# A gate behind the last value load, and mode 63 taken through the channel matrix by itself, in four column groups and two PSUM halves, with tables for units 0 to 3

## The chip, the cores and the metric

The kernel runs on one core of one Trainium2 chip. The metric is device time in microseconds (us) for one launch, from a call to its end. A profile is one execution recorded by the hardware; its span goes from the first to the last instruction of the program. In all texts PE is the matrix engine (PEld its weight loads), DVE the vector engine, ACT the scalar engine, POOL the GpSimd engine and SP the sync engine, which here only issues DMAs.

## The reference

Two layers stand one behind the other. The first is attention with a window of 128 and an ALiBi slope for each head; the second mixes the tokens in the frequency domain and applies a channel matrix.

```python
# q, k, v: (8 batches, 8 heads, 576 tokens, 64), fp32; w_r, w_i: (64, 512, 512); w_ch: (512, 512)
scores = where((rel >= 0) & (rel < 128), q @ k.T / 8 - slope * abs(rel), -1e9)
x = softmax(scores) @ v                       # laid out as (8, 576, 512)
X = rfft(x, axis=1)                           # over the tokens
Yr = einsum('bmd,mde->bme', Xr, w_r) - einsum('bmd,mde->bme', Xi, w_i)   # the first 64 modes
Yi = einsum('bmd,mde->bme', Xr, w_i) + einsum('bmd,mde->bme', Xi, w_r)
u = x + irfft(Yr + 1j * Yi, n=576)
out = u + maximum(u @ w_ch, 0)                # (8, 576, 512), fp32
```

The two mode weights are 64 x 2 matrices of 512 x 512 in fp32, 134 MB in all, and are read once. The output is 9.44 MB.

## The kernel before

**Attention** runs over 16 work units, a batch and a half of the heads each. `STAGE` is a list, written by hand, of steps with a lag; the loop over `stage` goes through it and so fixes the order of instructions on every engine. `cast("v", u)` turns the raw values into bf16 and then issues the load of unit u + 2 on SP's queue (`load`, lines 211 and 215). Behind each stage, POOL issues loads of mode weights: `AHEAD` says how many go into the `early` tiles in stages 1 to 13, `LATER` how many go into `spare` tiles, which are the raw buffers of q, k and v, in stages 12 to 15. Before the load of `AHEAD`, POOL copies one element of `x` that the stage before has just written, into `gate` (line 556). The copy has no other use than that POOL's queue waits there. The weights are cast from fp32 to bf16 on their way, which is why they are issued from POOL.

**The mode weights** are streamed next. The 64 modes go in 16 quads of four (`g`, with `LAST` = 15), and each quad has eight spots (`i`, with `k = 8 * g + i`). A spot of a quad multiplies weight tiles with the spectra in `XC` into the quad's accumulator `acc`, 32 columns of the matrix engine for each mode (line 861). `quad_end` scales and transposes a full accumulator into `YT`. Between the spots the kernel works on what is already there: `stream_spectra` takes finished spectra to rows `Z` and, through the channel matrix `wch`, to rows `ZW`; `project` and `augment` take all tokens through `wch` and add the first 32 modes (`XW`, and `x` in place). `warm` issues three matmuls that nobody reads. The last quad is split. Modes 60 to 62 are summed in `part_acc`, mode 63 in `acc`; `late_end` scales the first 96 rows into `yq`, sends them to rows of `Z` by small DMAs on POOL's queue (`patch`, line 639), and transposes them.

**The end** follows the last weight tile. Its mode's rows are scaled into `yq` by ACT, transposed and copied to `yT` (lines 935 to 940), taken through `wch` together with the other 96 rows (`late_channels`, line 592) into `yw`, and sent by `patch` to rows of `Z` and `ZW`. Then 18 output units follow, a pair of batches and 128 tokens each (two of them hold the last 64 tokens of four batches). For each unit PE fills an accumulator `mm` in `begin` (from `XW`) and `channels` (from `ZW`, with the inverse table `FT`) and an accumulator `yy` in `add_tokens` (from `x`) and `finish_tokens` (from `Z`). ACT writes `r = relu(mm)` in `activate`, DVE writes `o = yy + r` in `finish` (line 817), and SP sends `o` to the output (line 819). Units 0 and 1 (`FIRST`) do not wait for all of the small DMAs: `last_rows` multiplies the rows of `yq` or `yw` directly with a table `FM`, which holds the right rows of `FT` and zeros elsewhere. `FM` is filled with one memset and two DMAs on POOL's queue when the second set of weight buffers is opened. There are two slots of `mm` and `yy` from unit 1 on, and five buffers of `o`.

Of the kernel before, what the change touches and what calls it, by code (L numbers as in the profile page):

```python
# [402 lines left out]
def kernel(  # L403
# [87 lines left out]
    with ExitStack() as actx:  # L491
# [52 lines left out]
        for stage in range(min(lags), n + max(lags)):  # L544
# [8 lines left out]
            if stage in AHEAD:  # L553
                if stage:
                    b, g = at.units[stage - 1]
                    nc.gpsimd.tensor_copy(gate[:1, :1], x[:1, b, 0, 256 * g : 256 * g + 1])  # L556
                load_w(AHEAD[stage], early)
            if stage in LATER:
                load_w(LATER[stage], None)

    with ExitStack() as mctx:
# [8 lines left out]
        lctx, pctx = ExitStack(), ExitStack()  # L570
# [4 lines left out]
        def late_end(acc):  # L575
# [4 lines left out]
            patch([(nc.gpsimd, b) for b in range(2, B)], yq, lambda b: Z[:, b // 2, 1], 0, 6)  # L580
# [8 lines left out]

        def late_channels(zw, yT, yw, c):  # L590
            for et in range(4):
                nc.tensor.matmul(zw[:, c], lhsT=yT[:, et], rhs=wch[:, et, c],  # L592
                                 start=(et == 0), stop=(et == 3))
            nc.scalar.copy(yw[:, c], zw[:, c])
# [40 lines left out]
        def patch(todo, rows, dst, lo=0, hi=8):  # L635

            for queue, b in todo:
                r = 64 * (b % 2) + 8 * (LAST % 8)
                queue.dma_start(out=dst(b)[r + lo : r + hi],
# [6 lines left out]
        def spread(dst, half, b, hf, st, tok, rows=None):  # L646

            row = ROWS[(b % 2) ^ (1 - hf)]
            rows = ZW if rows is None else rows
# [77 lines left out]
        HALVES, FIRST = (0, 1, 2, len(units) - 1), (0, 1)  # L727
# [30 lines left out]
        def late_modes(dst, j, rows):  # L758

            b, st = units[j]  # L760
            for n in range(2):
# [4 lines left out]
                for row in range(2):  # L766
                    spread(dst[:, n], row, b + n, 1, st, row, rows)

        def channels(j):

            late_modes(mms[j][0], j, ZW)

        def last_rows(ps, j, rows):

            st = units[j][1]
            for n in range(2):
                nc.tensor.matmul(ps[:, n], lhsT=FM[:, n, st * P : (st + 1) * P], rhs=rows,  # L777
                                 start=False, stop=True, skip_group_check=True)
# [4 lines left out]
        def activate(j):  # L783

            if j in FIRST:
                last_rows(mms[j][0], j, heads["yw"])
# [13 lines left out]
        def finish_tokens(j):  # L800

            late_modes(yys[j][0], j, Z)

        def finish(j):

            b, st = units[j]
            if j == 0:
                last_rows(yys[0][0], 0, heads["yq"])
            else:
                if j not in yys:  # L810
                    take(j)
                add_tokens(j)
                finish_tokens(j)
            (yy, slot), r = yys.pop(j), rs.pop(j)
            o = heads["out"].tile([P, 2, DM], FP32, tag="o", bufs=5, name="o")
            for c in parts(j):
                nc.vector.tensor_tensor(out=o[:, c], in0=yy[:, c], in1=r[:, c], op=ALU.add)  # L817
# [12 lines left out]
            free.append(slot)  # L830

        quads, side, recycle = [], [], list(again)
        ZW = Z = XW = FM = FC = pairs = wch = w2 = None
        K1 = spot[again[-1]]
        for g in range(NM // 4):
# [5 lines left out]
            for i in range(8):  # L841
                k = 8 * g + i
                if i == 6 and g == LAST:
# [3 lines left out]
                    heads.update(mm=[head], yy=[head])  # L847
                    idle.append(0)
                    free.append(0)
                    begin(0)  # L850
                    channels(0)
                    take(0)
                    add_tokens(0)
                    finish_tokens(0)
                now = turns.pop(0) if turns and spot[turns[0][0]] == k else []
                for a in range(4):
                    for t in now:
                        m, ri = t // 2, t % 2
                        c0 = (a // 2 * 2 * NC + 16 * (1 - ri) + a % 2 * 8) * NM + m
                        into = part_acc if g == LAST and m < NM - 1 else acc  # L860
                        nc.tensor.matmul(  # L861
                            into[32 * (m % 4) : 32 * (m % 4) + 32],
                            lhsT=XC[:, c0 : c0 + 31 * NM + 1 : NM], rhs=wq[t][a],
                            start=(ri == 0 and a == 0), stop=(ri == (m > 0) and a == 3),
                            tile_position=(0, 32 * (m % 4)),
                        )
# [7 lines left out]
                if k == K1:  # L874
# [13 lines left out]
                    FM = right.tile([P, 2, 2 * P], BF16, name="FM")  # L888
                    nc.gpsimd.memset(FM, 0.0)
                    for b in range(2):  # L890
                        nc.gpsimd.dma_start(
                            out=FM.rearrange("(k v) b s -> k v b s", v=16)[:, b, b],
                            in_=FT[64 * b + 56 : 64 * b + 64, b, : 2 * P],
                        )
# [12 lines left out]
                elif g > LAST - 2 and k < 2 * NM - 1 or g == LAST - 2 and not side:  # L907
# [7 lines left out]
            if g == 7:  # L915
# [3 lines left out]
                side.append(partial(augment, len(units) - 1))  # L919
            elif g == LAST - 1:  # L920
# [3 lines left out]
        heads["out"] = mctx.enter_context(tc.tile_pool(name="res", bufs=6, reuse_waits="tile"))  # L924

        yq, yT = heads[LAST]
        zctx = ExitStack()
        zps = zctx.enter_context(tc.tile_pool(name="zps", bufs=1, space=PSUM))
        zl = zps.tile([P, DM], FP32, tag="z0", name="zl")
        nc.tensor.matmul(zl, lhsT=ident, rhs=wch[:, 0], start=True, stop=True)  # L930
        sides = (slice(0, DM // 2), slice(DM // 2, DM))
        trs = (lps.tile([P, 4, P], BF16, tag="tr", name="tr"),
               zps.tile([P, 4, P], BF16, tag="z1", name="tr1"))
        for i, c in enumerate(sides):
            nc.scalar.mul(yq[96:, c], acc[96:, c], 2.0 / S)
# [66 lines left out]
```

## Time and profile before

| | before |
|---|---|
| median of 3 runs | 444.19 us (438.96, 445.89, 444.19) |
| profiled execution | 441.24 us, span 439.4 us |
| mean granted PE clock | 0.847 |
| PE busy | 320.6 us (73%), 3509 matmuls |
| DVE, ACT, POOL busy | 183.7, 162.1, 87.0 us |
| DMA moved | 105.54 MB, 240 GB/s in the mean; POOL's queue 67.22 MB, SP's queue 37.79 MB |
| DMA share, 0 to 135, 141 to 401, 401 to 411, 411 to 437.9 us | 1.05, 1.06, 0.23, 0.97 |
| start of the last weight matmul; first output issue; last two output issues from | 405.27; 410.24; 432.65 us |

The page gives the busy time of each engine, the span in 40 slices, the DMA queues, the chain of work that ended last and the costliest groups of instructions. The DMA share is the busy part of the core's 16 transfer engines, and may come out a little over 1. Bytes are counted as written, so that a weight, read in fp32 and written in bf16, counts half. In a line of the timeline stand the start in us, the duration in us, engine, line of the kernel, operation, and output<-input with its shape; in brackets the idle time before it and what ended it.

### The profile page before, as it was taken

The numbers are of one execution on the slowest core, as the hardware profiler recorded it, in microseconds if no ns is written. First come the engines' busy times: TensorE is split into PE (matmuls) and PEld (weight loads), VectorE is DVE, ScalarE is ACT, GpSimd is POOL, SyncE is SP. The second block draws the span as 40 slices with busy tenths as digits, with TensorE's granted clock in tenths as the row PEclk, the third lists the DMA queues.
The fourth block names the chain that finished last, engine by engine and source line by source line (L and its number), as shares of the span: only waits on it lengthen the run. The fifth ranks groups of instructions, "written<-read, shape, count | busy, mean of one in ns | idle before, by whom it ended". The sixth has DMA issues, their size and how long they took to land. (4 is left out here: it accounts for less than half of the span.)

```text
span 439.4 us, 8314 instructions
## 1 busy us (share of the span) xinstructions
PE 320.6 (73%) x3509; PEld 177.6 (40%) x3509; DVE 183.7 (42%) x332; ACT 162.1 (37%) x211; POOL 87.0 (20%) x162
## 2 busy tenths in 40 slices
PE   4679899969796724553443387999889999698982
PEld 3357577647665411111111133444444444233430
DVE  7689699788783301010000022332222232122684
ACT  6769799987781000000000012323232323101780
POOL 8611011100323101322113111111111110012500
PEclk8679899999999965555555569999999999989997
DMA  8999999999999999999999999999999999997598
GB/s 280 306 329 301 300 292 312 266 302 283 266 224 213 216 214 213 214 213 214 214 213 215 214 214 214 214 215 215 214 214 215 216 213 214 214 215 135 199 368 306
DMA packets 52489, 105.54 MB, mean 240 GB/s; under 512 B 4052, under 2 KB 23396, under 8 KB 52452
## 3 DMA queue, kind: packets, MB, share of 16 engines
q0 software_dynamic: 18992, 67.22, 76.5%
q1 hardware_dynamic: 33460, 37.79, 26.3%
q8 instruction: 27, 0.44, 0.4%
q14 instruction: 10, 0.08, 0.0%
HBM read 162.53 MB, written 9.44 MB: 391 GB/s over the span
## 5 line engine op out<-in xcount | busy, mean ns | idle before, releaser
L861 PE MATMUL acc<-w,XC 128*32 128x512 bf16 x456 | 80.8, 485 | 68.8 <-DMA w<-in_moe_w_i_dram 35.4
L861 PEld LDWEIGHTS <-XC 128*32 128x32 bf16 x508 | 38.7, 148 | 110.1 <-issue 85.0
L297 ACT ACTIVATE att<-sc 128x1024 bf16<-128x1024 f32 x64 | 64.0, 1031 | 10.0 <-PE sc L287 10.0
L627 ACT CAST ZW<-zw 128x512 bf16<-128x512 f32 x8 | 4.7, 586 | 144.7 <-PE zw L625 144.7
L334 PE MATMUL av<-vb,att 128*128 128x132 bf16 (+1 forms) x576 | 38.4, 217 | 11.6 <-DVE x L350 8.8
L599 DVE TENSOR_SCALAR yq<-acc 128x512 bf16<-128x512 f32 x14 | 9.6, 687 | 82.2 <-PE acc L861 82.2
L334 PEld LDWEIGHTS <-att 128*128 128x128 bf16 x704 | 36.6, 98 | 17.2 <-DVE x L350 13.0
L693 PE MATMUL my<-wch,xT 128*64 128x512 bf16 x288 | 34.5, 381 | 5.8 <-ACT x L724 4.3
L702 ACT CAST XW<-my 128x512 bf16<-128x512 f32 x36 | 19.3, 589 | 50.5 <-PE my L650 50.5
L674 DVE COPY xT<-tr 128x1024 bf16<-128x1024 bf16 x18 | 12.5, 692 | 55.0 <-PE tr L672 55.0
L259 ACT COPY qkT<-tp 128x1152 bf16<-128x1152 bf16 x30 | 33.5, 1115 | 5.3 <-PE tp L253 4.5
L481 POOL DMA_DIRECT2D w<-in_moe_w_i_dram x23 | 16.3, 710 | 66.9 <-PE acc L861 44.2
L481 POOL DMA_DIRECT2D w<-in_moe_w_r_dram x22 | 15.6, 709 | 68.5 <-PE acc L861 48.1
L287 PE MATMUL sc<-qkT 64*64 64x256 bf16 (+2 forms) x640 | 25.7, 269 | 2.5 <-ACT qkT L259 1.6
L350 DVE TENSOR_TENSOR x<-av,rec 128x640 bf16<-128x640 f32 x32 | 26.4, 825 | 1.1
L693 PEld LDWEIGHTS <-xT 128*64 128x64 bf16 x288 | 17.1, 109 | 21.6 <-issue 9.2
L817 DVE TENSOR_TENSOR o<-yy,r 128x1024 f32<-128x1024 f32 (+1 forms) x22 | 21.5, 1025 | 4.8 <-DMA Z<-yq 2.6
L236 DVE CAST vb<-vr 64x1024 bf16<-64x1024 f32 x32 | 22.7, 708 | 0.4 <-DMA vr<-in_v_dram 0.2
L287 PEld LDWEIGHTS <-qkT 64*64 64x64 bf16 x640 | 14.8, 110 | 19.8 <-issue 16.5
L556 POOL COPY gate<-x 1x1 bf16<-1x1 bf16 x13 | 5.5, 423 | 86.2 <-DVE x L350 86.2
L724 ACT CAST x<-my 128x512 bf16<-128x512 f32 x18 | 10.6, 586 | 31.0 <-PE my L650 31.0
L274 PE MATMUL sc<-bias,ident 128*128 128x512 bf16 x64 | 20.7, 408 | 1.1 <-ACT att L297 1.1
(134 smaller groups left out, 431.0 us busy)
## 6 DMA issues: line engine op xcount, KB each, us to landing
w<-in_moe_w_i_dram POOLq DMA_DIRECT2D x23, 1024.0 KB, 35.8
w<-in_moe_w_r_dram POOLq DMA_DIRECT2D x22, 1024.0 KB, 35.7
qr<-in_q_dram SPq DMA_DIRECT2D x16, 576.0 KB, 9.2
kr<-in_k_dram SPq DMA_DIRECT2D x16, 576.0 KB, 8.2
vr<-in_v_dram SPq DMA_DIRECT2D x64, 128.0 KB, 7.6
w<-in_moe_w_r_dram POOLq DMA_DIRECT2D x16, 512.0 KB, 14.3
w<-in_moe_w_i_dram POOLq DMA_DIRECT2D x13, 512.0 KB, 24.0
out_dram<-o SPq DMA_DIRECT2D x13, 512.0 KB, 4.6
```

The source lines that it names most:

```text
L236: nc.vector.tensor_copy(self.vb[u % 2][row, :, :, :, W * half : W * half + D], src[row, :2])
L259: (self.nc.vector.tensor_copy if u < 2 and w == "q" else self.nc.scalar.copy)(dst.rearrange("q h (p j) -> q h p j", j=TPP), tp.rearrange(" ...
L274: nc.tensor.matmul(sc[:, e], lhsT=self.ident, rhs=self.bias[:, hv].rearrange("p j n -> p (j n)"), start=True, stop=False, skip_group_check ...
L287: nc.tensor.matmul(sc[64 * half : 64 * half + 64, e, j * 256 + c0 : j * 256 + c0 + n], lhsT=qkT[row, 1, h, k0 + j : k0 + P : 2], rhs=qkT[r ...
L297: self.nc.scalar.activation(self.att[u % 2][:, kt * 8 * P : (kt + 1) * 8 * P], sc.rearrange("p e n -> p (e n)"), AF.Exp, scale=1.0 / math. ...
L334: nc.tensor.matmul(bank[:, qt * W : qt * W + rhs[j].shape[1]], lhsT=att[:, o : o + P], rhs=rhs[j], start=(n == 0 and j == 0), stop=(n == l ...
L350: nc.vector.tensor_tensor(out=self.x[:, b, :, cs].rearrange("p t (h d) -> p h t d", h=2), in0=tiles[:, :, :, :D], in1=rec.unsqueeze(-1).br ...
L481: nc.gpsimd.dma_start(out=t.rearrange("p s a e -> p s (a e)"), in_=w[kinds.pop()][m : m + 2].rearrange("m (p a) e -> p m (a e)", a=4))
L693: nc.tensor.matmul(mm[ROWS[half]], lhsT=lhsT, rhs=wch[:, dt], start=(dt == 0), stop=False, skip_group_check=True,)
L702: nc.scalar.copy(XW[:, j, n], mms[n])
L817: nc.vector.tensor_tensor(out=o[:, c], in0=yy[:, c], in1=r[:, c], op=ALU.add)
L861: nc.tensor.matmul(into[32 * (m % 4) : 32 * (m % 4) + 32], lhsT=XC[:, c0 : c0 + 31 * NM + 1 : NM], rhs=wq[t][a], start=(ri == 0 and a == 0 ...
```

## The change

- In stage 13 POOL copies four elements of the last value unit's raw tile into `gate`, and issues the loads of `LATER[13]` behind it.
- `FM` and a second table `FM3` lie in the part of `YT` that is no longer used. `last_tables` fills them behind quad 11: a memset and four small copies on POOL, ten small DMAs on SP. `fold` is a matrix that adds up four groups of 32 rows.
- `late_end` gets a third part: the 96 rows of modes 60 to 62 go through `wch` ahead of the last weight tile, into `yw`, and their rows of `ZW` for batches 0 and 1 go by SP's queue. The three warming matmuls of spot 125 fall away.
- Mode 63 is summed in two halves of 256 columns in two PSUM tiles (`ends`); ACT scales one half and DVE the other. Then only its 32 rows go through `wch`: each of four column groups takes one quarter of the channels, and the four partial sums in `ywp` are added up by `FM3` for units 0 to 3, and by `fold` for everything else.
- Unit 0 adds `yq` and `yw` by tables; ACT copies its `yy` to `r`, and DVE takes the relu of `mm` in its sum. Units 1 to 3 (`FIRST`) take the rows of modes 60 to 62 from `ZW` (62 of 64 rows) and mode 63 from `FM3`.
- The order of the small DMAs changes; `o` has 7 buffers instead of 5, `r` has 4 instead of 6. Unit 2's `finish` comes before unit 3's `activate`.

```diff
+            if stage == n - 3:
+                nc.gpsimd.tensor_copy(gate[:1, :4], raw["v"][:1, (n - 1) % 2, 1, :, 0])
             if stage in LATER:
                 load_w(LATER[stage], None)
...
             heads[LAST] = yq, yT
-
-        def late_channels(zw, yT, yw, c):
+            yield
+            zl = heads["z"].tile([P, DM], FP32, tag="z0", name="zl")
             for et in range(4):
-                nc.tensor.matmul(zw[:, c], lhsT=yT[:, et], rhs=wch[:, et, c],
+                nc.tensor.matmul(zl[rows], lhsT=yT[:, et, rows], rhs=wch[:, et],
                                  start=(et == 0), stop=(et == 3))
-            nc.scalar.copy(yw[:, c], zw[:, c])
+            nc.scalar.copy(yw[rows], zl[rows])
+            patch(nc.sync, (0, 1), yw, ZW, 0, 6)
...
-        HALVES, FIRST = (0, 1, 2, len(units) - 1), (0, 1)
+        HALVES, FIRST = (0, 1, 2, len(units) - 1), (1, 2, 3)
...
             if j in FIRST:
-                last_rows(mms[j][0], j, heads["yw"])
+                if j not in mms:
+                    begin(j)
+                channels(j, 62)
+                last_rows(mms[j][0], j, ywp, FM3)
...
-            o = heads["out"].tile([P, 2, DM], FP32, tag="o", bufs=5, name="o")
+            o = heads["out"].tile([P, 2, DM], FP32, tag="o", bufs=7, name="o")
             for c in parts(j):
-                nc.vector.tensor_tensor(out=o[:, c], in0=yy[:, c], in1=r[:, c], op=ALU.add)
+                if j:
+                    nc.vector.tensor_tensor(out=o[:, c], in0=yy[:, c], in1=r[:, c], op=ALU.add)
+                else:
+                    nc.vector.scalar_tensor_tensor(out=o[:, c], in0=yy[:, c], scalar=0.0,
+                                                   in1=r[:, c], op0=ALU.max, op1=ALU.add)
...
+        def last_tables():
+
+            nc.gpsimd.memset(dead[:, : 10 * P], 0.0)
+            for et in range(4):
+                rows = slice(32 * et, 32 * et + 32)
+                nc.gpsimd.tensor_copy(fold[rows], ident[rows, rows])
+            by_row = [t.rearrange("(k v) b s -> k v b s", v=16) for t in (FM, FM3)]
+            for b in range(2):
+                top = 64 * b + 2 * HM - 8
+                nc.sync.dma_start(out=by_row[0][:, b, b], in_=FT[top : top + 8, b, :P])
+                for et in range(4):
+                    nc.sync.dma_start(out=by_row[1][2 * et : 2 * et + 2, b, b],
+                                      in_=FT[top + 6 : top + 8, b, : 4 * P])
...
                     begin(0)
-                    channels(0)
-                    take(0)
-                    add_tokens(0)
-                    finish_tokens(0)
+                    channels(0, 56)
+                    next(quads[0])
...
-                        into = part_acc if g == LAST and m < NM - 1 else acc
+                        into = [(acc, slice(0, DM))]
+                        if g == LAST:
+                            into = list(zip(ends, sides)) if m == NM - 1 else [(part_acc, slice(0, DM))]
...
-                elif g > LAST - 2 and k < 2 * NM - 1 or g == LAST - 2 and not side:
+                elif g > LAST - 2 and k < 2 * NM - 3 or g == LAST - 2 and not side:
                     warm()
...
+        nc.scalar.mul(yq[96:, sides[0]], ends[0][96:], 2.0 / S)
+        nc.vector.tensor_scalar_mul(yq[96:, sides[1]], ends[1][96:], 2.0 / S)
+        take(0)
+        add_tokens(0)
+        finish_tokens(0, 56)
+        tr = lps.tile([P, 4, P], BF16, tag="tr", name="tr")
+        for et in range(4):
+            nc.tensor.transpose(tr[:, et, 96:], yq[96:, et * P : (et + 1) * P], ident[96:, 96:])
+        nc.vector.tensor_copy(yT[:, :, 96:], tr[:, :, 96:])
+        patch(nc.sync, (0, 1), yq, Z)
+        patch(nc.gpsimd, range(2, 6), yq, Z, 6, 8)
+        (yy, slot), r = yys.pop(0), heads["out"].tile([P, 2, DM], FP32, tag="r", name="r")
+        last_rows(yy, 0, yq, FM, ns=(0,))
+        zp = [zps.tile([P, DM // 2], FP32, tag=f"z{i}", name=f"zp{i}") for i in range(2)]
         for i, c in enumerate(sides):
+            for et in range(4):
+                nc.tensor.matmul(zp[i][32 * et : 32 * et + 32], lhsT=yT[:, et, 96:],
+                                 rhs=wch[:, et, c], start=True, stop=True,
+                                 tile_position=(0, 32 * et))
+        nc.scalar.copy(r[:, 0], yy[:, 0])
+        last_rows(mms[0][0], 0, yw, FM, 96)
+        nc.vector.tensor_copy(ywp[:, sides[0]], zp[0])
+        nc.scalar.copy(ywp[:, sides[1]], zp[1])
+        last_rows(mms[0][0], 0, ywp, FM3)
+        zs = zps.tile([P, DM], FP32, tag="z0", name="zs")
+        nc.tensor.matmul(zs[96:], lhsT=fold, rhs=ywp, start=True, stop=True,
+                         tile_position=(0, 96))
+        last_rows(yy, 0, yq, FM, ns=(1,))
...
+        begin(1)
+        nc.scalar.copy(r[:, 1], yy[:, 1])
...
+        nc.scalar.copy(yw[96:], zs[96:])
+        patch(nc.gpsimd, (2, 3), yw, ZW)
+        patch(nc.gpsimd, (6, 7), yq, Z, 6, 8)
+        patch(nc.gpsimd, (0, 1), yw, ZW, 6, 8)
+        patch(nc.gpsimd, range(4, B), yw, ZW)
...
-        for j in (0, 1):
-            activate(j)
-            finish(j)
+        finish(0)
+        activate(1)
+        finish(1)
         activate(2)
-        for j in range(3, len(units)):
+        finish(2)
+        activate(3)
+        for j in range(4, len(units)):
             activate(j)
             finish(j - 1)
```

## The prediction

> **What bounds the kernel now.** I read the DMA rows of the page first. They are full from the first slices to the last but four: the transfer engines, not the compute engines, set the time, and what matters is where they are not full.
>
> ```profile
> DMA  8999999999999999999999999999999999997598
> GB/s 280 306 329 301 300 292 312 266 302 283 266 224 213 216 214 213 214 213 214 214 213 215 214 214 214 214 215 215 214 214 215 216 213 214 214 215 135 199 368 306
> ```
>
> Then I asked for the busy time of each engine in stretches of 2 us. The columns are the stretch, its length, then PE, PEld, DVE, ACT and POOL busy, granted clock, DMA share, GB/s.
>
> ```profile
> 400.00:402.00 2.00, 1.78 (x12) 0.74 (x15) 0.69 (x1) 0.59 (x1) 0.00 (x0) 1.00 0.88 159
> ...
> 404.00:406.00 2.00, 1.78 (x10) 0.69 (x9) 0.36 (x1) 0.32 (x2) 1.30 (x3) 1.00 0.14 23
> ...
> 408.00:410.00 2.00, 2.00 (x22) 0.76 (x15) 0.47 (x1) 1.28 (x4) 2.00 (x5) 1.00 0.08 17
> 410.00:412.00 2.00, 1.84 (x32) 0.86 (x25) 2.00 (x4) 1.46 (x4) 2.00 (x5) 1.00 0.48 164
> 412.00:414.00 2.00, 1.69 (x31) 0.83 (x28) 1.48 (x4) 2.00 (x4) 0.32 (x1) 1.00 0.95 324
> 414.00:416.00 2.00, 2.00 (x36) 1.06 (x29) 2.00 (x2) 2.00 (x3) 0.00 (x0) 1.00 0.87 318
> ```
>
> ```profile
> 416.00:424.00 8.00, 7.78 (x104) 3.41 (x103) 7.79 (x8) 6.76 (x8) 0.00 (x0) 1.00 1.03 378
> 424.00:426.00 2.00, 1.85 (x35) 0.89 (x28) 1.62 (x2) 1.79 (x3) 0.00 (x0) 1.00 0.89 327
> 426.00:437.00 11.00, 3.90 (x40) 1.26 (x31) 6.15 (x6) 2.78 (x4) 0.00 (x0) 0.88 1.03 380
> ```
>
> The reader is to see three parts: the weight stream, saturated to 401; a hole from there to 411, in which the last mode is turned into the first output; and the output, 18 units of 0.524 MB, saturated from 416 to 437. The last two fences give a rule. Before 416, 302, 324 and 318 GB/s over 1, 2 and 2 us (a finer window gives 302 for 411 to 412) moved 1.59 MB, just units 0 to 2. After it 8 x 378 + 2 x 327 + 11 x 380 = 7.86 MB, just the other 15 units. So the end follows **the moment at which unit 3's output is issued**, 0.9 us ahead of 416, as long as units 0 to 2 are through by then; after it the chip only drains, 21 us, then 2.4 us of closing.
>
> ```profile
> 413.14 0.33 SPq L819 DMA_DIRECT2D out_dram<-o  x1
> ...
> 415.06 0.39 SPq L819 DMA_DIRECT2D out_dram<-o  x1
> ```
>
> Next the matmul timeline of the hole, start, duration and operation:
>
> ```profile
> 405.27 0.38 PE L861 MATMUL acc<-w,XC 128*32 128x512 bf16 x1 [0.19 <-DMA w<-in_moe_w_i_dram]
> 405.58 0.39 PE L930 MATMUL zl<-wch,ident 128*128 128x512 bf16 x1
> 406.11 0.48 PE L937 MATMUL tr<-ident,yq 32*128 32x32 bf16 x4
> 406.61 1.16 PE L592 MATMUL zl<-wch,xT 128*128 128x256 bf16 x8
> 407.69 0.41 PE L753 MATMUL mm<-XW,ident 64*64 64x512 bf16 x4
> 407.94 0.39 PE L650 MATMUL mm<-ZW,FT 64*64 64x512 bf16 x4
> 408.25 0.60 PE L777 MATMUL mm<-F,FM 128*128 128x512 bf16 x2
> ```
>
> The last weight ends the wait at 405.27, and the first output is issued at 410.24. Starts of 512-column passes stand 0.214 apart (four L861 in 1.02 us, the last lasting 0.38); where the tile shape changes, L650 to L777, 0.31, so a change costs 0.095.
>
> **The gate.** At stage 13 POOL now copies from the last value tile before it issues the weight tiles of `LATER[13]`.
>
> ```profile
> 118.27 0.51 POOL L556 COPY gate<-x 1x1 bf16<-1x1 bf16 x1 [6.78 <-DVE x L350]
> 118.72 0.53 POOL L462 DMA_DIRECT2D w<-in_moe_w_i_dram  x1
> 119.24 0.54 POOL L462 DMA_DIRECT2D qr<-in_moe_w_r_dram  x1
> ...
> 123.47 0.54 POOL L462 DMA_DIRECT2D vr<-in_moe_w_i_dram  x1 [2.64 <-DMA vr<-in_v_dram]
> ```
>
> SP issues the last value rows at 117.8 and they take 5.8 us: 123.6. With a copy of 0.5 the load of 119.24 goes out at 124.1 to 124.3, five late; behind it in POOL's queue stand two more tiles, whose first readers come at 147.5, and then the `vr` tile of 123.47. The cover is the tile issued at 118.72, which lands 7.2 later, at 125.9. A small DMA on a free queue lands 1.6 us after its issue (the `ZW` rows at 409.7), so new data comes by 125.8: no hole if the landing tells when data moves, and up to 1.5 us of hole if its last 1.6 us is only reporting. In the saturated stream a hole moves everything behind it. What it could bring is less than its cover: the casts of those values at 127.7 follow other DVE work without a gap. I take +0.2; bounds 0 and +1.5.
>
> **Tables, and POOL.** `last_tables` puts on POOL a memset of 128x1280 (L519's 128x1024 took 0.96, so 1.2) and four small copies (gate copies 0.18 to 0.64), 3.6 us at most, ahead of the next weight loads, which land 35.7 us after issue: hidden; without that cover, 3.6. Ten small DMAs go to SP, which waits 228 us for the end anyway. Two `FM` DMAs leave POOL. Zero.
>
> **The last two weight tiles on PE.** Gone is one set of warming matmuls (0.82, ahead of a wait). Mode 63 is now summed in column halves, 16 passes of 256 columns for 8 of 512, and between its two tiles stand four passes for the other 96 rows (4 x 0.214 and two shape changes). A half pass would need 0.107, but the weight loads of 128x32 take 0.137 in this stage (groups by line from 384 to 410): I take 0.14 a pass. From 402.6: 8 x 0.14 + 0.86 + 0.19 + 7 x 0.14 puts the last pass at 405.75, its result (0.27) at 406.0 to 406.1 instead of 405.65. Loads that hide give 0; a start at 402.9, where it stood, gives +0.65. Taken: **+0.35**, since the queue no longer waits for the weights but they for it.
>
> **From there to the first output.** ACT and DVE take one half each of `yq`, 0.38 and about 0.42 (DVE's 512 columns take 0.69), for two of ACT in 0.65: saves 0.1. Eight 64-row passes for `yy` (0.43 and a shape change) fill that time to 406.7. Four transposes, 0.3; one copy of 128 columns, 0.25 (64 take 0.19), to 407.3. The eight zl passes of 1.16 become eight of 32 columns in four groups; rows of pairs in two groups already run two in the time of one (L861, eight in 1.09), so 0.4, to 407.75. ACT first copies `yy` (0.59), then its half of `ywp` (0.37): 408.2, as before. Two table passes (0.60): 408.85. The relu on ACT (0.60) falls away, since DVE takes it in (0.69 as its plain add): first issue 409.6, **0.64 earlier**.
>
> **From there to unit 3.** The second half waits for the fold (0.31), the `yy` pass (0.31 + 0.38, to 409.45), ACT's copy (0.6) and DVE (0.69): 410.85, as before. `begin(2)` needs that accumulator, so PE does units 2 and 3 behind it: activate, 4 groups of 0.214 and a shape change, 0.96; finish 0.53; activate 0.96; result of the last pass, 413.5. ACT's relu 1.03, DVE's sum 1.22 with hand-overs: issue at **415.8, 0.75 later** than 415.06. The two table passes for each of units 1 to 3 are what is new here: before, ACT was already at unit 3 at 412.47. Bounds: without the lateness and with half the shape changes hidden, -0.2; with the late start, +1.3.
>
> The other `o` buffers (7 for 5): DVE waited 1.3 us for a buffer, at full DMA; zero, at best the dip at 424, 2 x 53 GB/s or 0.3 us.
>
> Against this speaks a rule of the Trainium skill: "TensorEngine Tiling (Array Packing)", Key Properties, says that a change of tiling mode drains the TensorE. A true drain would start the next pass 0.38 behind the last, where the rows show 0.31; over some ten changes up to unit 3 the sum would be 0.7 us longer by the rule, and I keep the row.
>
> **Sum.** 0.2 + 0 + 0.75 = +0.95, say +1.0: span 440.4, and 442.2 for the profiled execution (441.24, of which 1.84 outside the span). The three runs lie from 438.96 to 445.89 with a median 2.95 above the profiled one; of the four executions the middle is 442.7, so I forecast **443.7**. The likeliest case's own effect is 0 to +2.2. A measurement of this kernel can tell about 2% (8.9 us) from no change.
>
> **Rivals.** *Late rows, slower.* Unit 4 needs `ZW` of batches 2 and 3 by DMA, issued only behind `yw`'s last copy: 410.6 and 411.1 on POOL. PE reaches unit 4 at 413.6, and unit 3's tokens stand behind it in PE's queue. In the profile such a DMA issued at 409.7 landed in 1.6 us, the two at 410.24 and 410.76, behind the first outputs, in 2.5 and 4.5. With 4.5 it lands at 415.6, then 0.3 + 0.43 + 1.22 to an issue at 417.65: 1.8 more, 445.5. It decides from a landing time of 2.5 us. Against it: fewer outputs stand ahead.
>
> By the Trainium skill, "DMA: Bandwidth & Descriptors", Queues, rings and completion order, each transfer engine takes turns between its queues packet by packet, so a small DMA would not be held; by that rule this rival costs nothing, and the 4.5 us of the trace speak against the rule.
>
> *Early start, faster.* The weight loads hide, and the 0.64 + 0.35 of the first output carries through because the 302 to 324 GB/s before 416 were short of data: 442.7 - 1.0 = 441.7. Against it: by 413.74 all 1.57 MB were issued and only some 0.9 moved, so what ran short was unit 3.
>
> *The gate opens a hole,* 1.5 instead of 0.2: 445.0. *The gate does nothing,* since the tile ahead of it is the one that shares the road with the values: 443.5, inside the forecast.
>
> **Chances.** Forecast, the idle gate included, 0.55; late rows 0.2; early start 0.15; hole 0.1. With the cases from 441.7 to 445.5 and the runs' own spread of some 3 us on each side the range is 438.5 to 448.5. Over 2% either way needs another cause than these, such as a half clock through the hole: 0.02 faster, 0.92 within, 0.06 slower.
>
> **What would show it.** Right: first issue near 409.6, second near 410.9, unit 3's near 415.8; passes of 256 columns 0.14 apart; DMA share at 1.0 from 118 to 130. Wrong: unit 3's issue before 415.06 (chain too long), or PE waiting for `ZW` at unit 4 (late rows), or a dip near 124 to 126 (hole). An end that does not move with unit 3's issue would overthrow the rule.

## The result and the profile after

The change makes the kernel slower. Its median is 443.91 us (442.15 to 448.86, 14 runs) against 439.29 us for the kernel before in the same comparison (438.51 to 445.89, 14 runs); the ratio is 1.0090, interval 1.0065 to 1.0114, which is +4.0 us (2.9 to 5.0). This ratio, like those below, leaves out executions in a slower state, such as the one of 448.86 us, and is not that of the medians, which lie 4.6 us apart. The profiled execution took 443.43 us with a span of 441.7 us.

The DMA rows of the page after, in 40 slices of 11 us:

```profile
DMA  8999999999999999999999999999999999996598
GB/s 286 316 319 306 275 318 296 308 300 275 242 190 213 214 214 214 214 214 214 215 212 215 214 214 214 214 215 215 214 213 215 214 214 215 215 213 123 189 355 323
```

Two places differ. The slice from 121.5 us shows 190 GB/s where the kernel before has 224; and the tail holds 123, 189, 355 where before it held 135, 199, 368. The finer windows (the stretch, its length, then PE, PEld, DVE, ACT, POOL busy, granted clock, DMA share, GB/s) show where:

```profile
124.00:126.00 2.00, 2.00 (x38) 1.49 (x36) 1.32 (x3) 1.97 (x3) 1.95 (x4) 1.00 0.65 89
...
408.00:410.00 2.00, 1.99 (x14) 0.61 (x14) 0.70 (x2) 0.68 (x2) 1.21 (x3) 1.00 0.07 13
410.00:412.00 2.00, 2.00 (x24) 0.51 (x24) 1.39 (x3) 1.71 (x4) 1.06 (x2) 1.00 0.57 203
412.00:414.00 2.00, 1.92 (x23) 0.60 (x23) 1.88 (x3) 1.47 (x3) 2.00 (x5) 1.00 0.57 195
414.00:416.00 2.00, 0.81 (x14) 0.64 (x17) 0.00 (x1) 0.83 (x2) 1.74 (x5) 1.00 0.84 295
416.00:418.00 2.00, 1.92 (x35) 1.03 (x30) 1.69 (x2) 2.00 (x3) 0.48 (x1) 1.00 0.40 135
```

From 124 to 126 the core moves 89 GB/s; in the kernel before it moved 216 there. And from 412 to 418, where before the output ran at 324, 318 and then 378 GB/s, it now runs at 195, 295 and 135. In 414 to 416 PE is busy for 0.81 us of 2 and DVE not at all. PE's timeline names the reason (start, duration, operation, in brackets the idle time before it and what ended it), and SP's gives unit 3's issue:

```profile
412.97 0.60 PE L781 MATMUL mm<-XC,YT 128*128 128x512 bf16 x2
413.51 0.41 PE L757 MATMUL mm<-XW,ident 64*64 64x512 bf16 x4
415.19 0.58 PE L654 MATMUL mm<-ZW,FT 64*64 64x512 bf16 x4 [1.27 <-DMA ZW<-F]
415.40 0.58 PE L757 MATMUL yy<-x,ident 64*64 64x512 bf16 x4
```

```profile
417.56 0.39 SPq L830 DMA_DIRECT2D out_dram<-o  x1
```

Unit 3's table passes are done at 413.5. The next work in PE's queue is unit 4, whose second pass needs the small DMA rows of `ZW` for batches 2 and 3; only behind it stand the passes for unit 3's tokens, at 415.40. POOL issued those rows at 410.94 and 411.49, and they landed at 415.15 and 415.32, 4.2 and 3.8 us later. The trace keeps sixteen reports for each of these landings: fifteen had come by 412.99 for the first row and by 413.19 for the second, so that it is one late report that holds each row for another 2.1 us.

The other place is POOL's queue in stage 13:

```profile
118.25 0.53 POOL L462 DMA_DIRECT2D w<-in_moe_w_i_dram  x1
123.31 0.18 POOL L559 CAST gate<-vr 1x4 bf16<-1x4 f32 x1 [4.53 <-DMA vr<-in_v_dram]
123.82 0.54 POOL L462 DMA_DIRECT2D qr<-in_moe_w_r_dram  x1 [0.33 <-issue]
```

The load that the kernel before issued at 119.24 goes out at 123.82, and the next one at 124.35 instead of 119.76.

**One table carries the account.** All from the profiled executions: the MB of weights landed from POOL's queue by 150 us (summed over its packets), the start of the last weight matmul, unit 3's issue and the span's end, with the two distances.

| kernel | MB at 150 | last weight matmul | unit 3 issued | between | to the end |
|---|---|---|---|---|---|
| before | 13.24 | 405.27 | 415.06 | 9.79 | 24.3 |
| before, 7 `o` buffers | 13.53 | 403.79 | 413.58 | 9.79 | 24.3 |
| before, with the gate | 12.88 | 405.90 | 415.69 | 9.79 | 24.3 |
| after | 12.94 | 405.86 | 417.56 | 11.70 | 24.1 |
| after, no gate | 13.52 | 405.08 | 416.90 | 11.82 | 24.2 |
| after, fold first | 12.82 | 406.29 | 416.27 | 9.98 | 23.9 |
| no gate, fold first | 13.70 | 403.37 | 414.40 | 11.03 | 24.2 |
| no gate, unit 3 first | 13.44 | 404.49 | 414.55 | 10.06 | 24.4 |
| no gate, fold first, row split off | 13.32 | 404.13 | 414.10 | 9.97 | 23.8 |
| the same, unit 3 first | 12.76 | 407.11 | 417.07 | 9.96 | 24.1 |
| the same, unit 3 in halves | 13.41 | 404.41 | 414.05 | 9.64 | 24.2 |
| the same, gate one tile later | 13.61 | 403.49 | 413.47 | 9.98 | 23.8 |
| the same, gate two tiles later | 12.44 | 408.29 | 418.26 | 9.97 | 24.0 |
| no gate, rows on ACT's queue | 13.50 | 403.95 | 415.65 | 11.70 | 23.5 |

"The same" stands in four rows for the kernel of the row above them, "no gate, fold first, row split off". The expectations quoted below count from the landing of the last weight tile; the table counts from the matmul on it, which begins 0.04 to 0.4 us later, and 1.5 later in the changed kernel without the gate, where PE was not through with its own work.

The last column is nearly one number: the end follows unit 3's issue. The loss has two parts: the stream of weights ends later, and unit 3 follows it later by 1.9 us. Between the second row and the fourth: 2.07 + 1.91 - 0.18 = 3.8 us of span (437.9 to 441.7), close to the +4.0 of the timed runs. The profiled execution of the kernel before had itself a late stream (13.24 MB against 13.53), and so it hides most of the first part: its own span is only 2.3 us shorter than the one after.

### The profile page after: what moved, and what is told of

The parts are those of the page before. It is cut to its first block, busy times and chain, and to the rows that moved or that the text cites. A ratio compares the mean times of both kernels' runs of the same rounds, so it can differ in the third digit from the quotient of the medians.

```text
span 441.7 us, 8353 instructions
## 1 busy us (share of the span) xinstructions
PE 322.6 (73%) x3524; PEld 179.0 (41%) x3524; DVE 185.3 (42%) x333; ACT 162.9 (37%) x211; POOL 89.2 (20%) x168
## 4 chain that ended last, share of the span: by engine, by line
DMA 68%; PE 12%; DVE 9%; issue 5%; ACT 3%; POOL 1%; SPq 0%; DVEq 0%; POOLq 0%; ACTq 0%
DMA w<-in_moe_w_r_dram 43%; DMA w<-in_moe_w_i_dram 15%; DMA qr<-in_q_dram 5%; PE av L334 3%; DMA vr<-in_v_dram 2%; DMA kr<-in_k_dram 2%; PE xt L371 2%; PE tp L253 1%; DVE att L308 1%; DVE x L350 1%; DVE o L825 1%; DVE vb L236 1%; DVE q L241 1%; PE acc L897 1%; DMA ZW<-F 1%
## 5 line engine op out<-in xcount | busy, mean ns | idle before, releaser
L897 PE MATMUL acc<-w,XC 128*32 128x512 bf16 (+1 forms) x464 | 81.3, 482 | 65.5 <-DMA w<-in_moe_w_r_dram 32.2
L697 PE MATMUL my<-wch,xT 128*64 128x512 bf16 x288 | 35.6, 388 | 10.0 <-DVE x L729 4.3
L825 DVE TENSOR_TENSOR o<-yy,r 128x1024 f32<-128x1024 f32 (+1 forms) x20 | 20.0, 1056 | 3.2 <-PE yy L654 2.3
```

The costliest lines, as they stand in the source:

```text
L697: nc.tensor.matmul(mm[ROWS[half]], lhsT=lhsT, rhs=wch[:, dt], start=(dt == 0), stop=False, skip_group_check=True,)
L897: nc.tensor.matmul(to[32 * (m % 4) : 32 * (m % 4) + 32], lhsT=XC[:, c0 : c0 + 31 * NM + 1 : NM], rhs=wq[t][a][:, c], start=(ri == 0 and a ...
```

## The experiments

The theory: a hole behind the gate, and two late rows. Its rival: all of the loss is in the longer chain of tables at the end, and the gate costs nothing.

**Take away the gate; put it into the kernel before.**

```diff
 # no gate: the changed kernel without
-            if stage == n - 3:
-                nc.gpsimd.tensor_copy(gate[:1, :4], raw["v"][:1, (n - 1) % 2, 1, :, 0])
 # before, with the gate: the same two lines added to the kernel before
```

> The changed kernel without POOL's copy from the last value tile; all else as changed. Theory (hole and late rows): in the changed kernel's trace the three loads behind the copy go out at 124.35 to 125.39 instead of 119.24 to 120.28, and the DMA share falls to about 0.45 and 0.63 in the two microseconds from 124; that is about 1.0 us of missing work, and everything behind it moves. Without the copy the share stays near 1.0 from 118 to 130 and the time falls by 1.0 to 1.5 us against the changed kernel: about 442.6. First rival (the tail alone): the hole is made up later, the time stays within 0.4 us of the changed kernel. Second rival (the copy also helps the casts of the values): the time rises, by up to 0.5.

> The kernel before plus POOL's copy from the last value tile, nothing else. Theory (hole and late rows): a hole of about 1.0 us near 124 to 126, time +1.0 to +1.5 us against the kernel before, about 440.5. First rival (the tail alone): within 0.4 us of the kernel before. Second rival (the copy helps the values): faster by up to 0.5.

Without the gate 441.48 us, ratio to before 1.0038 (1.0005 to 1.0071): 2.3 us under the changed kernel. The kernel before with the gate 441.89 us, 1.0041 (1.0006 to 1.0076): 1.8 us over it. So the gate is slower in both surroundings. The 1.0 to 1.5 us expected lie a little under both values, but well inside their uncertainty (0.3 to 3.3 us for the second). The windows of the kernel before with the gate, and of the changed kernel without it:

```profile
124.00:126.00 2.00, 2.00 (x37) 1.49 (x36) 1.45 (x3) 1.68 (x2) 1.87 (x4) 1.00 0.56 74
```

```profile
124.00:126.00 2.00, 1.49 (x34) 1.18 (x31) 1.25 (x4) 2.00 (x3) 0.00 (x0) 1.00 1.02 204
```

The hole comes and goes with the two lines. From 118 to 130 the DMA share is 1.10 in the kernel before and 1.09 in the changed one without the gate, 0.98 and 0.99 with it: 1.2 to 1.4 us of the transfer engines' time are lost there, close to the 1.0 expected. The table suggests why the price may differ between executions. Without a gate the weights stand at 13.2 to 13.7 MB at 150 us, but for one execution that is told of below; with it at 12.8 to 12.9 in all three kernels that have it at its place. The stream is held to the values, whether the attention ran ahead or not. The most extreme is the changed kernel with the fold first: the value row that its gate waits for was issued at 114.8, over two us earlier than in the other two, and the gate still opened only at 123.8, with the DMA share at 0.17 and 0.31 in the two stretches from 122 to 126. Here, too, reports were late: fourteen of the row's sixteen had come by 120.79, the others at 122.47 and 123.65.

**Send the two rows out before the first output.**

```diff
-        last_rows(mms[0][0], 0, ywp, FM3)
         zs = zps.tile([P, DM], FP32, tag="z0", name="zs")
         nc.tensor.matmul(zs[96:], lhsT=fold, rhs=ywp, ...)
+        nc.scalar.copy(yw[96:], zs[96:])
+        patch(nc.gpsimd, (2, 3), yw, ZW)
+        last_rows(mms[0][0], 0, ywp, FM3)
```

> The changed kernel with the fold of mode 63's channel rows, its copy and the two small DMAs of batches 2 and 3 moved ahead of the table passes of unit 0, so that these DMAs go out about 1.5 us earlier, near 409.4 instead of 410.94, ahead of the first output. Theory (hole and late rows): they land near 411 to 412.5 instead of 415.15 and 415.32; PE reaches unit 4's second pass without waiting; unit 3's output goes out near 415.9 instead of 417.56, and the time falls by about 1.7 us against the changed kernel, though the first output goes out about 0.35 later. Rival (the chain of tables alone costs): PE and ACT are the bound up to unit 3 either way, unit 3's output stays past 417 and the time within 0.4 us of the changed kernel, or higher by the later first output. Second rival (the end does not hang on unit 3's issue): unit 3 goes out earlier and the time stays.

> The changed kernel with both of the others: no copy from the last value tile, and the fold with its two DMAs ahead of unit 0's table passes. Theory (hole and late rows): the two gains add, 2.7 to 3.2 us against the changed kernel, about 441, and some 1 us over the kernel before is left, which is the longer chain of tables up to unit 3. Rival (the tail alone): the same time as with the fold moved alone. Second rival (nothing of this): the time of the changed kernel.

With the gate 442.12 us, 1.0044 (1.0009 to 1.0079), 2.0 under the changed kernel; without it 440.57, 1.0020 (0.9986 to 1.0053). With the gate the rows were issued at 409.91 and 410.46, landed 1.6 and 2.4 us later, and PE went on at unit 4 without a wait, with unit 3's tokens 0.2 us behind:

```profile
414.08 0.39 PE L654 MATMUL mm<-ZW,FT 64*64 64x512 bf16 x4
414.29 0.39 PE L757 MATMUL yy<-x,ident 64*64 64x512 bf16 x4
```

Unit 3 follows the last weight matmul by 9.98 us instead of 11.70. Without the gate the second row went out 0.1 us behind the first output (407.54 and 407.44), took 4.6 us, and PE waited again; hence 11.03, and part of the gain is missing. With the gate it had stood just as far behind the first output (410.46 and 410.36) and taken 2.4 us, so a row at the same place close to the outputs can be in time or late.

**Move the second row to SP's queue; put unit 3 ahead of unit 4 on PE.** Three kernels, none with the gate.

```diff
 # row split off (with the fold first)
-        patch(nc.gpsimd, (2, 3), yw, ZW)
+        patch(nc.gpsimd, (2,), yw, ZW)
+        patch(nc.sync, (3,), yw, ZW)
 # unit 3 first
         activate(3)
-        for j in range(4, len(units)):
+        finish(3)
+        activate(4)
+        for j in range(5, len(units)):
```

> No gate, the fold ahead of unit 0's table passes, and the row of batch 3 on SP's queue, ahead of the first output there, instead of second on POOL's queue. Theory (a small DMA is late when outputs are in flight before its last packet has moved): both rows, out before the first output, land 1.6 to 1.8 us after their issue, where the row of batch 3 took 4.6 us when it went out 0.1 us behind the first output; PE meets unit 4 without a wait, and unit 3's output goes out some 0.6 us earlier, 10.3 to 10.7 us behind the last weight instead of 11.3. Time about 440.0, 0.6 under the kernel with the row on POOL. Rival (POOL's queue itself makes the second of two rows late): the row on SP lands in time as well, so the times agree with the theory, but then the row of batch 2 alone on POOL must be no later with outputs in flight. Second rival (one slow transfer engine, whatever stands in the queues): one of the two rows is late again.

> The changed kernel without the gate, and with unit 3's tokens put ahead of unit 4's channel passes on PE, so that unit 3 no longer stands behind the wait for the two late rows. Theory (late rows): the rows land late as before, about 4.3 us after issue; unit 3's output goes out about 1.7 us earlier counted from the last weight's landing (11.6 instead of 13.3 us), unit 4's only about 0.6 earlier, since it still waits. The time falls against the kernel with the gate alone taken out by 0.6 (if unit 4 now sets the end) to 1.7 us (if unit 3's issue does): 439.8 to 440.9. Rival (the DMA engines, not the order on PE, hold the first outputs back): unit 3's output goes out earlier, but the time stays within 0.4 us.

> All three: no gate, the fold first with the row of batch 3 on SP's queue, and unit 3's tokens ahead of unit 4's channel passes on PE. Theory: unit 3's output goes out about 0.9 us earlier than without the reordering, some 9.4 to 9.8 us behind the last weight, which is the 9.83 of the kernel before or a little under it; time 439.0 to 439.8, the kernel before within 0.5 us. Rival (output is limited by what units 0 to 2 have moved by then): unit 3 goes out earlier and the time stays at about 440.0.

With the row split off 440.04 us, 1.0008 (0.9981 to 1.0036): no difference from the kernel before can be told, and PE meets no wait. Neither row is late, so an engine that is slow whatever stands in the queues is not seen here. A row on POOL's queue with outputs in flight was late again (issued at 409.31, landed 3.7 us later, the other fifteen reports in by 411.47), so which of queue and traffic does it is left to the last run below. Unit 3 first without the fold: unit 3 is 1.8 us nearer to the weights (10.06 for 11.82) while the rows still take 3.7 to 4.1 us, so it was the order on PE that carried their lateness to unit 3. The time, 440.96 us, 1.0027 (1.0001 to 1.0053), is 0.5 under the kernel without the gate, at the low end of what was expected; the interval is too wide to tell 0.5 from nothing.

The third did not do what was expected: unit 3 follows the last weight matmul by 9.96 us as without the reordering (9.97), and the time is 442.00 us, 1.0044 (1.0011 to 1.0077). With no wait for rows left, unit 3 hangs on ACT's relu and DVE's sum behind PE's last table pass, and the order on PE is worth nothing. That explains why nothing was gained. The loss lies 280 us earlier:

```profile
132.41 1.39 DVE L236 CAST vb<-vr 64x1024 bf16<-64x1024 f32 x2 [6.58 <-DMA vr<-in_v_dram]
```

```profile
132.00:134.00 2.00, 0.00 (x0) 0.00 (x0) 1.38 (x2) 0.00 (x0) 0.00 (x0) 1.00 0.44 88
134.00:136.00 2.00, 0.00 (x0) 0.00 (x0) 0.86 (x3) 0.00 (x0) 0.74 (x2) 0.75 0.24 19
```

In this execution the last value rows, issued at 114 to 117, came so late that DVE's cast waited 6.58 us: of the row issued at 115.48 fifteen reports had come by 122.92, the last at 132.29. POOL's next weight loads write into the buffer which that cast frees, and stood for 11.3 us. The hole is larger than the gate's: 12.76 MB at 150 us. The profile of the kernel with the row split off has the same on a smaller scale: fifteen reports by 121.85, the last at 128.64, a wait of 3.12 us at the cast, 13.32 MB. So there is something that a gate could guard against, which the profile of the kernel before did not show. That the gate does so is not shown: of the twelve times of the kernel before with the gate four are above 442.9, one of them 596.57. The twelve times of this kernel lie in two groups, six below 441.1 and six above 442.9; of the other kernels without a gate none to three of twelve are in the upper one, of the kernel before four of 35 in the same comparison and eight of 29 in the next. That the upper times are all of this kind was not shown, since only one execution of a kernel is profiled.

**Can the gate be had without its hole?** On the kernel with the row split off, the gate put back one tile and two tiles later.

```diff
 # one tile later
+            if stage == n - 3:
+                load_w(1, None)
+                nc.gpsimd.tensor_copy(gate[:1, :4], raw["v"][:1, (n - 1) % 2, 1, :, 0])
+                load_w(LATER[stage] - 1, None)
+            elif stage in LATER:
+                load_w(LATER[stage], None)
 # two tiles later: the copy behind load_w(LATER[stage], None)
```

> The same kernel (no gate where the change has it, fold first, row split off) with the gate put back one weight tile later: one of stage 13's two late tiles is issued ahead of POOL's copy, the other behind it. Theory (the gate's price is a hole because only one tile covers it, and its worth is that value rows cannot be held up behind weight tiles): two tiles of 0.52 MB, 4.9 us at 0.214 MB per us, cover the wait for the rows, so the loss of 0.66 MB by 150 us shrinks to 0.1 MB or less, and DVE's cast of the last values does not wait; about 440.0 to 440.5, without the slower third of the executions that the kernels without a gate show (443 to 445). Rival (any gate costs, since its copy sees the rows only when the last straggling packet is reported): 441 to 442, with the hole a little later.

> As the run before, with the gate behind both of stage 13's late tiles: three tiles cover the wait. Theory: no hole, the weights as far along at 150 us as without a gate (13.4 MB or more), values on time in most executions; 439.5 to 440.3, the same as or slightly below the kernel without a gate in the median, by the executions that are not held up. Rival (two tiles ahead of the rows are enough to hold them up): as many executions at 443 to 445 as without a gate.

One tile later: 440.03 us, 1.0027 (0.9991 to 1.0064). Its profile shows no hole (13.61 MB at 150 us, gate open at 121.7) and a cast without a wait; but two of its twelve times are above 443, and its median is that of the kernel without a gate, so a net use was not found. Two tiles later: 441.00 us, 1.0029 (0.9992 to 1.0066), and the rival came true: two of its times are above 443, where the kernel without the gate has one. In the profiled execution, the slowest of the twelve at 444.04, the rows were held up all the same, and the gate turned the delay into POOL's:

```profile
130.09 0.70 POOL L561 CAST gate<-vr 1x4 bf16<-1x4 f32 x1 [11.96 <-DMA vr<-in_v_dram]
```

**Three smaller questions.** The seven buffers alone; unit 3's relu and sum in halves; the late rows from ACT's queue.

```diff
-            o = heads["out"].tile([P, 2, DM], FP32, tag="o", bufs=5, name="o")     # kernel before
+            o = heads["out"].tile([P, 2, DM], FP32, tag="o", bufs=7, name="o")
-        HALVES, FIRST = (0, 1, 2, len(units) - 1), (1, 2, 3)                        # row split off
+        HALVES, FIRST = (0, 1, 2, 3, len(units) - 1), (1, 2, 3)
-        patch(nc.gpsimd, (2, 3), yw, ZW)                                            # changed, no gate
+        patch(nc.scalar, (2, 3), yw, ZW)
```

> The kernel before with seven output buffers for five, nothing else. Theory (the transfer engines are full when DVE waits for a buffer): no change, within 0.4 us of the kernel before; the stream of weights and the start of the output as in the profile of before. Rival (the dip of the DMA share near 424 is a want of buffers): 0.3 us faster and no dip.

The buffers do nothing: 439.73 us, 0.9994 (0.9976 to 1.0011).

> No gate, fold first with the row of batch 3 on SP's queue (the kernel of the run with that row split off), and unit 3's relu and sum in two halves, as units 0 to 2 have them. There unit 3's output hung on one relu of 1.03 and one sum of 1.22 behind PE's last table pass, and the DMA share fell to 0.41 in the microsecond before its data moved. Theory (the end follows the moment unit 3's data is issued, and that is set by ACT and DVE): the first half goes out about 1.1 us earlier, 9.1 instead of 10.2 us behind the last weight, the dip is filled, time 0.3 to 0.6 us lower, about 439.6. Rival (what units 0 to 2 left is not the limit, the transfer engines' start is): the first half goes out earlier and the time stays within 0.2 us.

Unit 3's first half went out 9.64 us behind the last weight matmul, 0.33 nearer and not 1.1, and the time stayed: 440.31 us, 1.0017 (0.9987 to 1.0047). Two things took the rest, and either alone would have taken nearly as much. DVE's sum of that half waited for PE's passes over unit 3's tokens, which stand behind unit 4's channel passes, and ended at 413.82; and SP, whose issue of unit 1's second half took 1.74 us where 0.33 to 0.39 is usual, did not come to it before 414.05:

```profile
410.95 1.74 SPq L828 DMA_DIRECT2D out_dram<-o  x1
...
413.13 1.29 DVE L823 TENSOR_TENSOR o<-yy,r 128x512 f32<-128x512 f32 x2 [0.68 <-PE yy L652]
```

Unit 2's first half was summed at 411.86 and issued at 412.80, and the DMA share fell to 0.15 from 412 to 413.

> The changed kernel without the gate, with the two late rows of batches 2 and 3 issued from ACT's queue instead of POOL's, at the same place behind unit 0's outputs. Theory (the transfer engines have the outputs' packets in hand, and the row is complete only when the slowest of them has come to its packets): they still land 3 us or more after issue, and PE waits for them at unit 4. Rival (POOL's queue alone is slow while others run): they land 1.6 to 2.2 us after issue and PE does not wait, though ACT has the two issues to make.

One run, 441.10 us. The rows were late on this queue too, as the theory had it: issued at 408.78 and 409.98, they were reported in full at 413.00 and 413.42, 4.2 and 3.4 us later, and again all reports but one of each had come by 411.36 and 412.00. So POOL's queue alone is not the reason. PE hardly waited at unit 4 all the same (0.1 us, until the report of 413.42), since it got there 1.3 us later (412.91 - 403.95 = 8.96 us behind the last weight matmul, for 412.72 - 405.08 = 7.64), because ACT, which has unit 1's relu to do, paid for the issues:

```profile
408.78 1.77 ACTq L640 DMA_DIRECT2D ZW<-F  x2
410.68 2.06 ACT L798 ACTIVATE r<-mm 128x512 f32<-128x512 f32 x4 [1.93 <-PE mm L779]
```

Unit 1's first half went out at 412.03, and unit 3 as late as with the rows on POOL (11.70). The rows' packets moved from 410.47 to 411.37, but for the last few at 412.11 to 412.23. Rows were late from either queue when outputs were in flight, and in time from POOL's and SP's when they went out ahead of them; why just one report of a row lags stays open.

## Why the prediction was right and wrong

**The number was met by two errors that cancel.** The forecast was 443.7 and the median is 443.91. But the base was 442.7, the middle of four executions from two groups of times, and the kernel before stands at 439.29; and the effect was +1.0, and is +4.0 (4.6 by the medians). That 443.7 was met is luck. Ten of the 14 times of the kernel before lie from 438.5 to 439.5; of the four that the base was taken from only one did, and the profiled one, with its late stream, was 2 us above.

**The step that failed first: the gate at +0.2, with 1.5 as its bound.** Measured +1.8 in the kernel before and 2.3 in the changed one, with some 1.5 us either way, and 1.2 to 1.4 us lost by the transfer engines from 118 to 130. The prediction had all of the parts: the issue at 124.1 to 124.3 (123.82), one tile of cover that lands at 125.9 (125.49), no gain at the casts (127.23, no gap). It then had to choose whether a landing tells when data moves, and chose nearly that it does. The trace after says it does not: the tile "landed" at 125.49 and the road was already at 0.42 from 124 to 125. Whether more than the bound was lost is not clear of the noise. If it was, the likely reason is that the bound was worked out for this execution's timing; in others the values come earlier, the stream could have run ahead further, and the gate takes that away too. "The gate opens a hole" was a rival at 0.1.

**The rival that came true on top: late rows, which the sum had at nothing.** Sent out a microsecond earlier, they gave back 2.0 us. Its working was right almost to the digit: landing after 4.5 us (4.2 and 3.8), unit 3's issue at 417.65 (417.56), 1.8 us (11.70 - 9.98 = 1.72). Only its chance, 0.2, was wrong, and the argument against it, "fewer outputs stand ahead", did not hold. The Trainium skill, "DMA: Bandwidth & Descriptors", Queues, rings and completion order, was quoted with the rule that engines take turns packet by packet, by which the rows would not be held. Of the two rows' 16 data packets 15 had moved by 412.8, and fifteen of each row's sixteen reports had come by 412.99 and 413.19, but the last came at 415.15 and 415.32. The same page, under "Why a DMA increments its semaphore by 16 and not by 1", states that a DMA counts as landed only when every engine that it was spread over has reported. The trace agrees with that, and it is the sentence that bears on this case.

**The chain of tables at +0.75.** Behind the last weight pass it was right: 415.8 - 405.75 = 10.05 us predicted to unit 3, 9.98 measured where the rows come in time, 9.79 before. What was too dear is the 0.48 by which that last pass was to come later. Counted from the landing of the last weight tile it begins 0.04 us behind it in the kernel before, and 0.22 to 0.26 behind it in the changed kernels whose PE waits for the weights: 0.2 later, and +0.4 in place of +0.75 at unit 3. A half pass was taken at 0.14; it is (1.03 less 0.27 for the last one's duration) / 7 = 0.109, so its weight load hides:

```profile
403.08 1.03 PE L897 MATMUL acc<-w,XC 128*32 128x256 bf16 x8 [0.30 <-DMA w<-in_moe_w_r_dram]
404.05 1.06 PE L594 MATMUL zl<-wch,xT 128*96 128x512 bf16 x4
405.04 1.09 PE L897 MATMUL acc<-w,XC 128*32 128x256 bf16 x8
```

By the rule of a TensorE drained at each change of tiling mode, quoted in the prediction, the way to unit 3 would have been 10.75; 9.98 stands with the row.

**What held.** First output 409.6 predicted and 409.60 seen, the second 410.85 and 410.80 (3.74 us from the last weight pass to the first, for 3.85; that the times on the clock agree as well is partly luck, since the profiled execution of the kernel before had a late stream of its own); nothing from the buffers, and no sign of a cost of the tables on POOL or of a gain by an early start; and the rule that the end follows unit 3's issue, 23.5 to 24.4 us ahead of the span's end in fourteen profiles.

**The sentence on what can be told apart was wrong.** About 2% was named as the smallest difference that a measurement of this kernel can tell from no change. Fourteen runs of each told 0.9%, with 0.25% either way. The chances were laid on "within 2%", and so said little about the sign.

## What to carry to other kernels

A copy that holds a DMA queue behind another transfer is paid in the time from that transfer's report to the next data on the road, so count the cover in bytes left to move, not in landing times, and ask what the queue could have fetched ahead in an execution that is luckier than the one profiled. Ahead of a saturated stretch, issue the small transfers that later work waits for before the first large one, and look at what stands behind their reader in an engine's order. A base for a forecast needs enough executions to show the groups in which the times lie: here the middle of four was 3.4 us off. And look at when each part of a transfer was reported: one late report of sixteen held the work here, at both ends of the kernel.

## What the runs showed of the hardware

- In the kernel without the gate and with the fold first, a small DMA issued 0.1 us behind the first output took 4.6 us to land, the one issued 0.56 us earlier 1.6 us; with the gate one at the same place took 2.4 us. In the changed kernel, where both were behind outputs, fifteen of the sixteen reports of each came within 2.1 us of the issue, and the last 2.1 us after them. From ACT's queue, with outputs in flight, the rows took 4.2 and 3.4 us, again by one late report each.
- One late report at full load held value rows issued at 114 to 117 us until DVE could start at 132.4 in one execution and 128.8 in another. In a third, with three weight tiles issued ahead of the gate, most reports were late and DVE started at 130.1. In the kernel before the last value rows take 5.8 to 7.0 us from issue to landing.
- In thirteen of the fourteen profiles SP's issue of one of the fourth to sixth outputs took 0.63 to 1.74 us, against 0.33 to 0.45 for the others; in three of them the DMA share then fell to 0.25, 0.19 and 0.15 for a microsecond. Why was not tried.
